# Threshold attention and a feed-forward block on one core: weight masks on VectorE, small copies on ScalarE, transposes ahead of the products with v, and two extra products a slot

## The chip, the cores and the metric

The kernel runs on one core of a Trainium2 chip. The metric is the device time of one execution in microseconds (us); lower is better. For profiled executions I also quote the span, which is some 2 us shorter than the time.

## The reference

Eight batches, eight heads, 576 rows of 64. Attention keeps the scores that lie within tau of the row's maximum. Its output is laid out as rows of 512 and goes through a normalised feed-forward block with 2048 hidden features.

```python
scores = scale * np.matmul(q, k.transpose(0, 1, 3, 2))
thresh = np.max(scores, axis=-1, keepdims=True) - tau
scores = np.where(scores >= thresh, scores, -1000000000.0)
scores = scores - np.max(scores, axis=-1, keepdims=True)
attn = np.exp(scores)
attn = attn / (np.sum(attn, axis=-1, keepdims=True) + 1e-09)
attn_out = np.matmul(attn, v)
# ... x = attn_out as rows of 512 ...
xn = (x - mu) / np.sqrt(var + 1e-06) * g_ln
out = x + np.maximum(xn @ w_ch1, 0.0) @ w_ch2
```

The feed-forward weights arrive as float64, which the kernel reads as pairs of 32-bit words and turns into float32 itself, in 32 chunks of 512 columns.

## The kernel before

The work is cut into **units** (one batch, two heads) of five **slots** (128 rows of queries each; the fifth has the last 64 rows of both heads). There are 32 units and 160 slots, numbered from 0. The program order is fixed by hand: `at_point(3 * n + i, ...)` hangs a piece of work on a point of slot n.

```python
for u in range(len(units)):
    for j in range(PTS):                     # five slots
        scs = scores(u, j)                   # TensorE
        es, thr = exponentials(scs)          # VectorE maximum, ScalarE exp
        conversion.carry()
        run(3 * n)                           # what hangs on this point
        ...
        weights(scs, es, thr)                # VectorE masking, GpSimd scaling
        conversion.end()                     # weight chunk: last step
        run(3 * n + 1)
        ...
        conversion.begin(2 if 20 <= n < 24 else 1)
        if blocks:                           # batches 1 to 7: through DRAM
            at_point(3 * n + 4, ...)         # turn_blocks: et -> scr
            if j in (1, 3, 4):
                at_point(3 * n + 7, ...)     # fetch: scr -> em, er
                at_point(3 * n + 12, ...)    # values_of: pv
        else:                                # batch 0: TensorE transposes
            at_point(3 * n + 3, turn_weights, u, j, es)
            if j in (1, 3, 4):
                at_point(3 * n + 6, lambda u=u, j=j: values_of(u, j, rounds.pop(u)))
        n += 1
```

In batch 0 (slots 0 to 19) the attention weights are transposed on TensorE (tile tp, and tr for the last 64 columns), then copied to em and er:

```python
def turn_weights(u, j, es):
    # ... em, er, tr allocated ...
    for h in range(2):
        # ... four transposes into tp, one into tr ...
        nc.scalar.copy(em[:, h, :, o : o + 128], tp)
    for h in range(2):
        # ...
        nc.vector.tensor_copy(er[r, o : o + 128], tr[r, h])
```

In the other seven batches VectorE transposes blocks into et, four DMAs carry et to a scratch tensor in DRAM (scr), and others bring it back as em and er. All these DMAs are issued by one queue, SyncE's. The products pv (v with em, then with er) wait for that round trip.

A weight chunk goes through ScalarE (Square, Sign and a scaled Identity) and is finished by GpSimd with a product. Three small constants serve that.

```python
g_sb = consts.tile([128, NK], F32, name="g_sb")
g_half = consts.tile([128, NK], F32, name="g_half")
half_sb = consts.tile([128, 1], F32, name="half_sb")
tiny_sb = consts.tile([128, 1], F32, name="tiny_sb")
ident = consts.tile([128, 128], F32, name="ident")
# ... weights, then the pools ins (q, k, v) and att (e, em, er, et) behind ...
```

## Time and profile before

| | before |
|---|---|
| median of 3 runs | 1567.52 us (1562.31 to 1567.53) |
| span of the profiled run | 1561.5 us |
| TensorE busy | 1477.1 us, 95% |
| mean granted TensorE clock | 0.965 of full |
| slots 0 to 25 (210.86 us) | loop of waits, clock 0.76 from 8 to 170 us |
| from slot 26 on (1339.9 us) | TensorE full, clock 1.00 |

First TensorE's timeline ahead of slot 13, a fourth slot of its unit (start us, duration us, engine, line, operation, tiles, count; in brackets the idle time before and what ended it; in all timelines here, lines between those shown are left out):

```profile
106.47 3.46 PE L416 MATMUL pv<-em,v_in 128*64 128x256 f32 x16
109.76 0.60 PE L416 MATMUL pv<-er,v_rest 128*64 128x256 f32 x4
112.70 0.30 PE L347 MATMUL tr<-ident,e 128*64 128x128 f32 x1 [1.75 <-ACT x L427]
```

and VectorE's in that slot:

```profile
113.58 0.59 DVE L354 COPY er<-tr 64x128 f32<-64x128 f32 x2 [2.00 <-PE tr L349]
114.20 0.82 DVE L309 SCALAR_TENSOR_TENSOR e<-sc,thr,e 128x576 f32<-128x576 f32 x1
```

The product pv goes first, ScalarE carries it out, only then can tr be written (1.75 us of waiting), and VectorE, whose small copy stands ahead of the masking in its queue, waits 2.00 us for tr. The next scores wait for the masking. Over the first 240 us that wait is (us in total, times, longest):

```profile
PE sc L278 <- DVE e L309: 37.1, 23, 3.9
```

### The profile page before, as it was taken

The numbers are of one execution on the slowest core, as the hardware profiler recorded it, in microseconds if no ns is written. First come the engines' busy times: TensorE is split into PE (matmuls) and PEld (weight loads), VectorE is DVE, ScalarE is ACT, GpSimd is POOL, SyncE is SP. The second block draws the span as 40 slices with busy tenths as digits, with TensorE's granted clock in tenths as the row PEclk, the third lists the DMA queues.
The fourth block names the chain that finished last, engine by engine and source line by source line (L and its number), as shares of the span: only waits on it lengthen the run. The fifth ranks groups of instructions, "written<-read, shape, count | busy, mean of one in ns | idle before, by whom it ended". The sixth has DMA issues, their size and how long they took to land.

```text
span 1561.5 us, 17868 instructions
## 1 busy us (share of the span) xinstructions
PE 1477.1 (95%) x5686; PEld 714.8 (46%) x5686; DVE 808.6 (52%) x1548; ACT 460.8 (30%) x786; POOL 513.9 (33%) x774
## 2 busy tenths in 40 slices
PE   5777699999999999999999999999999999999998
PEld 3444344444444444444444444444444444444443
DVE  5666676666556655665566555655656551001001
ACT  5666664212321232123211421133113320210200
POOL 4656673333223322333233323332333222100000
PEclk8867599999999999999999999999999999999999
DMA  5333387787667776777667767776777665001001
GB/s 141 96 87 94 106 199 165 166 182 163 152 156 173 165 167 152 161 152 190 141 150 167 162 156 159 157 174 150 159 154 169 149 139 121 7 3 17 7 7 20
DMA packets 701452, 204.37 MB, mean 131 GB/s; under 512 B 632752, under 2 KB 697264, under 8 KB 701360
## 3 DMA queue, kind: packets, MB, share of 16 engines
q1 hardware_dynamic: 698960, 202.95, 57.1%
q8 instruction: 46, 0.75, 0.2%
q10 hardware_dynamic: 2368, 0.30, 0.1%
q14 instruction: 46, 0.38, 0.1%
q0 software_dynamic: 32, 0.00, 0.0%
HBM read 119.41 MB, written 83.76 MB: 130 GB/s over the span
## 4 chain that ended last, share of the span: by engine, by line
PE 79%; SPq 6%; DVE 5%; DMA 4%; POOL 2%; ACT 2%; issue 2%; POOLq 0%; DVEq 0%; ACTq 0%
PE p L494 31%; PE p L536 26%; PE pv L416 10%; PE sc L278 10%; DMA em<-scr 4%; DVE e L309 2%; SPq L103 2%; SPq L479 1%; SPq L372 1%; ACT e L297 1%; PE tp L338 1%; SPq L117 1%; DVE neg L290 1%; SPq L121 1%; POOL w L230 1%
## 5 line engine op out<-in xcount | busy, mean ns | idle before, releaser
L494 PE MATMUL p<-xc,w 128*128 128x512 f32 x1152 | 518.6, 600 | 12.5 <-DVE xc L455 9.8
L536 PE MATMUL p<-hidden,w 128*128 128x512 f32 x1152 | 513.1, 597 | 0.0
L297 ACT ACTIVATE e<-sc,neg 128x576 f32<-128x576 f32 x288 | 199.9, 737 | 602.7 <-DVE neg L290 588.5
L290 DVE TENSOR_REDUCE neg<-sc 128x1 f32<-128x576 f32 x288 | 206.2, 751 | 309.7 <-PE sc L278 309.0
L494 PEld LDWEIGHTS p<-xc,w 128*128 128x128 f32 x1152 | 213.1, 190 | 270.0 <-issue 244.9
L536 PEld LDWEIGHTS p<-hidden,w 128*128 128x128 f32 x1152 | 214.2, 190 | 263.2 <-issue 260.5
L315 POOL TENSOR_SCALAR e<-e,den 128x576 f32<-128x576 f32 x288 | 218.3, 764 | 257.1 <-DVE den L313 241.1
L309 DVE SCALAR_TENSOR_TENSOR e<-sc,thr,e 128x576 f32<-128x576 f32 x288 | 225.4, 816 | 70.4 <-ACT e L297 69.0
L293 POOL TENSOR_SCALAR thr<-neg,low_sb 128x1 f32<-128x1 f32 x288 | 76.0, 264 | 501.2 <-DVE neg L290 500.3
L278 PE MATMUL sc<-kT,qT 64*128 64x288 f32 x1024 | 188.3, 459 | 39.4 <-DVE e L309 30.9
L501 ACT ACTIVATE hidden<-p 128x512 f32<-128x512 f32 x144 | 86.0, 598 | 352.6 <-PE p L494 352.5
L416 PE MATMUL pv<-em,v_in 128*64 128x256 f32 (+1 forms) x1536 | 167.1, 353 | 6.1 <-DMA em<-scr 5.9
L278 PEld LDWEIGHTS sc<-kT,qT 64*128 64x128 f32 x1024 | 103.2, 198 | 148.8 <-issue 93.7
L365 DVE STREAM_TRANSPOSE et<-e 128x1152 f32<-128x1152 f32 x112 | 152.9, 1365 | 0.5
L416 PEld LDWEIGHTS pv<-em,v_in 128*64 128x64 f32 x1536 | 93.6, 145 | 85.4 <-issue 43.4
L471 POOL TENSOR_TENSOR o<-o,x 128x512 f32<-128x512 f32 x36 | 45.7, 1268 | 216.5 <-DVE o L470 216.5
L470 DVE TENSOR_TENSOR o<-p,rb 128x512 f32<-128x512 f32 x36 | 24.6, 683 | 161.5 <-PE p L536 150.0
L416 PE MATMUL pv<-er,v_rest 128*64 128x256 f32 (+1 forms) x384 | 54.3, 332 | 0.0
L510 POOL TENSOR_TENSOR ss<-ss,sq 128x512 f32<-128x512 f32 x27 | 34.4, 1273 | 60.1 <-ACT sq L508 60.1
L427 ACT COPY x<-pv 128x256 f32<-128x256 f32 (+3 forms) x120 | 32.0, 288 | 46.3 <-PE pv L416 42.9
L278 PE MATMUL sc<-kT,q_diag 128*128 128x288 f32 x128 | 37.7, 418 | 6.3 <-DVE e L309 6.2
L255 DVE STREAM_TRANSPOSE qT<-q_in 128x256 f32<-128x256 f32 x56 | 21.6, 423 | 41.6 <-POOL q_in L248 41.6
(68 smaller groups left out, 694.6 us busy)
## 6 DMA issues: line engine op xcount, KB each, us to landing
scr<-et SPq DMA_DIRECT2D x224, 288.0 KB, 4.4
em<-scr SPq DMA_DIRECT2D x112, 512.0 KB, 5.0
hidden<-in_moe_w_ch_dram SPq DMA_DIRECT2D x32, 512.0 KB, 3.8
q_in<-in_q_dram SPq DMA_DIRECT2D x128, 72.0 KB, 4.3
out_dram<-ot SPq DMA_DIRECT2D x144, 64.0 KB, 1.9
k_in<-in_k_dram SPq DMA_DIRECT2D x124, 72.0 KB, 2.6
v_in<-in_v_dram SPq DMA_DIRECT2D x64, 128.0 KB, 3.6
scr_rest<-et SPq DMA_DIRECT2D x112, 72.0 KB, 4.6
```

The source lines that it names most:

```text
L278: nc.tensor.matmul(sc[:, c, :HALF], lhsT=lhsT, rhs=kT[rows, c * HALF : (c + 1) * HALF], start=True, stop=True,)
L290: nc.vector.tensor_reduce(out=neg[:, i : i + 1], in_=sc[:, :, :HALF], axis=AXL.XY, op=ALU.max, negate=True)
L293: nc.gpsimd.tensor_scalar(out=thr[:, i : i + 1], in0=neg[:, i : i + 1], scalar1=-1.0, scalar2=low_sb, op0=ALU.mult, op1=ALU.add,)
L297: nc.scalar.activation(es[:, i].rearrange("p (c n) -> p c n", c=2), sc[:, :, :HALF], func=AF.Exp, bias=neg[:, i : i + 1],)
L309: nc.vector.scalar_tensor_tensor(out=e2, in0=sc[:, :, :HALF], scalar=thr[:, i : i + 1], in1=e2, op0=ALU.is_ge, op1=ALU.mult, accum_out=den ...
L315: nc.gpsimd.tensor_scalar(out=es[:, i], in0=es[:, i], scalar1=den[:, i : i + 1], scalar2=1.0, op0=ALU.mult, op1=ALU.mult,)
L365: nc.vector.transpose(et[:, :, :, j % 2], es.rearrange("p h (n c) -> p h n c", c=32))
L416: nc.tensor.matmul(pv[64 * h : 64 * h + 64, :n], lhsT=vt[:, c, h, :] if c < J else vr[:, h, :], rhs=em[:, h, c, :n] if c < J else er[:, :n ...
L471: nc.gpsimd.tensor_tensor(out=o, in0=o, in1=groups[g][:, m], op=ALU.add)
L494: nc.tensor.matmul(p1, lhsT=w1_sb[c][:, d * 128 : (d + 1) * 128], rhs=xc[:, c, :], start=(c == 0), stop=(c == NK - 1),)
L501: nc.scalar.activation(hidden[:, d], p1, func=AF.Relu)
L536: nc.tensor.matmul(p2, lhsT=w2_sb[d][:, m * 128 : (m + 1) * 128], rhs=hidden[:, d], start=(d == 0), stop=(d == ND - 1),)
```

## The change

The intent is to relieve GpSimd and ScalarE of the weight masks, to end VectorE's wait for tr, and to keep TensorE's clock up in the first 21 slots. One VectorE comparison-and-multiply replaces Sign, Identity and GpSimd's product. The er copies move to ScalarE. In batch 0, pv moves behind the slot's transposes (point 3n+7 for 3n+6). Two products of 128x512 whose result is never read end each of slots 0 to 20. The three small constants go, since nothing uses them.

```diff
-    g_half = consts.tile([128, NK], F32, name="g_half")
-    half_sb = consts.tile([128, 1], F32, name="half_sb")
-    tiny_sb = consts.tile([128, 1], F32, name="tiny_sb")
 ...
-            nc.scalar.activation(y, y, func=AF.Sign, bias=tiny_sb)
-            nc.scalar.activation(y, y, func=AF.Identity, scale=gh, bias=gh)
 ...
-            nc.gpsimd.tensor_tensor(out=chunks[i][0], in0=a, in1=y, op=ALU.mult)
+            dst, _, gi = chunks[i]
+            nc.vector.scalar_tensor_tensor(
+                out=dst if gi is None else a, in0=y, scalar=(1.0625 * 2.0**-15) ** 2, in1=a,
+                op0=ALU.is_ge, op1=ALU.mult,
+            )
+            if gi is not None:
+                nc.gpsimd.tensor_scalar(
+                    out=dst, in0=a, scalar1=g_sb[:, gi : gi + 1], scalar2=1.0,
+                    op0=ALU.mult, op1=ALU.mult,
+                )
 ...
-                nc.vector.tensor_copy(er[r, o : o + 128], tr[r, h])
+                nc.scalar.copy(er[r, o : o + 128], tr[r, h])
 ...
+    def keep_busy(u):
+        idle = ps_ff.tile([128, TOK], F32, tag="ff", name="idle")
+        for _ in range(2):
+            nc.tensor.matmul(
+                idle, lhsT=avg_sb, rhs=turned[u][1][:, :TOK], start=True, stop=True,
+            )
 ...
+            if n < 21:
+                keep_busy(u)
 ...
-                    at_point(3 * n + 6, lambda u=u, j=j: values_of(u, j, rounds.pop(u)))
+                    at_point(3 * n + 7, lambda u=u, j=j, tw=rounds_at: values_of(u, j, tw[0]))
```

More of the change, by code (lines that the diff above doesn't have):

```diff
@@ L136 @@
     nc.vector.memset(avg_sb, 1.0 / DM)
-    nc.vector.memset(half_sb, 0.5)
-    nc.vector.memset(tiny_sb, -(1.0625 * 2.0**-15) ** 2)
     nc.vector.tensor_scalar(
@@ L151 @@
     nc.gpsimd.dma_start(out=g_sb, in_=g_ln.rearrange("(c p) -> p c", p=128))
-    nc.gpsimd.tensor_scalar(
-        out=g_half, in0=g_sb, scalar1=0.5, scalar2=1.0, op0=ALU.mult, op1=ALU.mult
-    )
     WC = 512
@@ L214, in begin @@
             )
-            gi = chunks[i][2]
-            gh = half_sb if gi is None else g_half[:, gi : gi + 1]
-            nc.scalar.activation(y, y, func=AF.Sign, bias=tiny_sb)
-            nc.scalar.activation(y, y, func=AF.Identity, scale=gh, bias=gh)
             made[i] = (a, y, r)
@@ L353, in turn_weights @@
                 o = (j % 2) * 128
-                nc.vector.tensor_copy(er[r, o : o + 128], tr[r, h])
+                nc.scalar.copy(er[r, o : o + 128], tr[r, h])
             else:
-                nc.vector.tensor_copy(er[r, :64], tr[r, h, r])
+                nc.scalar.copy(er[r, :64], tr[r, h, r])
+        return em, er, n
     def turn_blocks(u, j, es):
@@ L671 @@
             else:
-                at_point(3 * n + 3, turn_weights, u, j, es)
+                rounds_at = []
+                at_point(
+                    3 * n + 3,
+                    lambda u=u, j=j, es=es, tw=rounds_at: tw.append(turn_weights(u, j, es)),
+                )
                 if j in (1, 3, 4):
-                    at_point(3 * n + 6, lambda u=u, j=j: values_of(u, j, rounds.pop(u)))
+                    at_point(3 * n + 7, lambda u=u, j=j, tw=rounds_at: values_of(u, j, tw[0]))
             n += 1
```

## The prediction

> **What bounds the kernel now.** I read the page's forty slices first, then three long stretches cut where the slices change, then the groups of instructions of the first 240 us, and last the timeline of single slots. The slices:
>
> ```profile
> PE   5777699999999999999999999999999999999998
> DVE  5666676666556655665566555655656551001001
> PEclk8867599999999999999999999999999999999999
> ```
>
> TensorE is full from the sixth slice on; in the first five it is neither full nor at full clock. The stretches (columns: length, then busy time with instruction counts of PE, PEld, DVE, ACT, POOL, then clock, DMA share, GB/s):
>
> ```profile
> 8.46:166.85 158.39, 115.92 (x557) 70.72 (x557) 104.96 (x232) 102.30 (x167) 97.28 (x119) 0.76 0.39 106
> 166.85:209.63 42.78, 27.15 (x82) 12.59 (x82) 30.73 (x56) 27.25 (x43) 28.53 (x32) 0.71 0.48 135
> 209.63:1561.50 1351.87, 1334.04 (x5048) 631.48 (x5048) 670.77 (x1253) 329.98 (x576) 384.98 (x611) 1.00 0.60 134
> ```
>
> The third stretch is 1334.04 of 1351.87 us busy at clock 1.00: it is matmuls in a fixed order, and the change adds none there. Only the first two, 201 us, can move. Nobody is full in them, so a loop of waits sets the pace, and the groups name it:
>
> ```profile
> L278 PE MATMUL sc<-kT,qT 64*128 64x288 f32 x192 | 59.3, 593 | 39.4 <-DVE e L309 30.9 <-DVE qT L259 8.5
> L354 DVE COPY er<-tr 64x128 f32<-64x128 f32 x32 | 9.2, 288 | 25.4 <-PE tr L349 25.2
> L356 DVE COPY er<-tr 64x64 f32<-64x64 f32 x8 | 1.8, 222 | 11.8 <-PE tr L349 11.8
> L347 PE MATMUL tr<-ident,e 128*64 128x128 f32 x20 | 7.0, 349 | 10.2 <-ACT x L427 10.2
> ```
>
> Scores wait for the masking on VectorE (L309); VectorE in turn stood 25.4 + 11.8 = 37.2 us ahead of the small copies (er) for TensorE's transposes, which, where a product pv came before them in the slot, waited for ScalarE to carry pv out. A slot (VectorE's first maximum to the next slot's) is on average, over slots 5 to 19 by place in the unit of five: 7.6 (6.63, 9.54, 6.62), 7.4, 10.9 (this one ends with the transposes of the next unit's q and k), 7.2 and 5.0 us, 38.2 a unit.
>
> **What the Trainium skill says.** (1) "TensorE: Matmul & The Clock Gate", Part 1: the array runs at half clock unless a free-running window of 3413 ns was busy. The trace agrees: read by single microseconds the clock is 1.00 or 0.50, and all its changes in the first 220 us lie on one grid of 3.413 us. (2) The same page's Part 4 says transposes do not count as busy. The trace disagrees: a window of transposes and little else kept the clock,
>
> ```profile
> 147.27:150.69 3.42, 1.77 (x14) 1.03 (x10) 1.42 (x3) 2.33 (x5) 1.78 (x3) 1.00 0.00 0
> 130.21:133.62 3.41, 0.94 (x7) 0.71 (x7) 1.56 (x5) 3.07 (x7) 3.41 (x5) 0.98 0.00 0
> 188.23:191.64 3.41, 3.17 (x4) 1.17 (x4) 3.41 (x6) 0.93 (x2) 3.41 (x4) 0.52 0.81 284
> ```
>
> while 0.94 us (second line) lost it: the next window is at 0.50. Over all windows to 220 us I fit, as an estimate, some 1.25 us of full-array work to keep the clock, with the scores of 64 rows counting about half; to win it back a window must be nearly full (third line, 3.17 us of 128x512 products, then warm). (3) "SBUF — State Buffer", section "SBUF: two separate sides": a VectorE operation with two SBUF inputs and a GpSimd operation exclude each other on a shared port. The trace agrees: L206 takes 0.69 us alone and 1.11 us beside L315. (4) "PSUM — Partial Sum Buffer", "Engine vs sequencer instructions": ScalarE's queue is strictly first in, first out. The trace shows every em copy after that slot's exponentials; this decides the sign below.
>
> **The change part by part.** *Mask.* ScalarE loses two operations a chunk (0.72 + 0.81 us), 32 times; it is not on the loop. GpSimd loses the product w (1.33 us) and gets a one-input scaling for the 16 w1 chunks (est. 0.7 us, from L315's 0.76 for 576). VectorE gets one two-input operation of 512: like L206, est. 1.1 us beside L315, and it is on the loop, once per chunk. *Small copies.* VectorE loses 0.59 us a slot and the wait before it. Its own loop is then maximum 1.42, exponential 0.21 more, masking 1.56, reciprocal with gaps 0.3, weight mask 1.1, next chunk 0.42 + 1.1: 6.0 us; with the turn of q and k 9.25; 5.05 for the single-sided fifth slot. *Idle products.* Each is two records of 128x512; L494's fourteen records in 6.17 us give 0.44 us a record in a stream, so two products are 1.75 us warm and about twice that cold. *Order.* In a slot TensorE now has scores, transposes, pv, idle products, next scores. pv takes the PSUM buffer of the slot's first transposes (rings of two, taken in order of first use; the wait of tr for x above confirms that order), so it waits for the em copy, which stands behind both exponentials. From the maximum N: exponentials end at N+2.1, em copy N+2.7, pv from N+2.75, 2.2 us warm, idle 1.75, scores 1.24 and 0.25 to reach VectorE: N+8.2 (N+7.9 ahead of the fifth slot, whose scores are shorter; N+6.75 where pv is the 64-column one).
>
> Before pv TensorE now stands idle: about 6 us in the fourth slot (maximum late after the turn), 3.5 in the first, 1.5 in the second. By the window rule the first two start pv cold, the fourth always, the first four times in five; the 7.7 us of pv and idle products end it after 3.4 to 6.8 us, mean 5.1, of which half is lost: 2.5 us x 1 and 2.4 x 0.8 = 1.9; the second slot 0.3.
>
> | slot in unit | before | after |
> |---|---|---|
> | 1st, pv 256 | 7.6 | 8.2 + 1.9 = 10.1 |
> | 2nd, pv 64 | 7.4 | 6.75 + 0.3 = 7.05 |
> | 3rd, turn | 10.9 | 9.25 |
> | 4th, pv 256 | 7.2 | 7.9 + 2.5 = 10.4 |
> | 5th | 5.0 | 5.05 |
> | unit | 38.2 | 41.85 |
>
> Three units: 3 x 3.7 = +11. The first unit was 34.1 us and has one pv slot: I get 36.6, +2.5. Slot 20 was 12.6 (VectorE waited for GpSimd's product w, and pv was cold) and becomes 10.1: -2.5. Slot 21 was 11.4 and becomes 3.2 + 0.3 + two masks 2.2 + a transpose 1.36 + two chunks 2.65 = 9.7: -1.7, because the waits of 2 to 3 us for w are gone. From slot 22 to 209.63 two masks more a slot (+2.2 each) against waits removed come out even, and the cold stretch after the 3.2 us gap at 206 should go: -3. Later masks may cost 1. Sum: 11 + 2.5 - 2.5 - 1.7 - 3 + 1 = +7 us.
>
> **Rivals.** (a) VectorE becomes the loop and pv hides: 6.0 + 6.0 + 9.25 + 6.0 + 5.05 = 32.3 us a unit, 3 x 5.9 = 18 us less; with 3 less in the first unit, slot 20 at 7.25 (5.4 less) and the same 3.7 after it, about 1538. For it: the 37.2 us of waits are real. Against: pv and idle products (3.95 us) follow the exponentials in the first and fourth slots and end after VectorE is ready. (b) The clock stays low, because the gaps outlast windows: cold pv slots run 2.75 + 4.2 + 3.5 + 2.5 = 13 us, others 2 us more, some 10 us a unit, 1607. For it: the gaps of 3.5 and 6 us. Against: the idle products alone are 3.5 us cold and follow pv, a full window. (c) The products warm the array everywhere, without loss: 37.2 us a unit, about 1558. (d) The masks (12 after slot 20) delay the first FFN group: VectorE is 30.73 of 42.78 us busy there; up to 5 us more.
>
> **Range and chances.** The sum gives 1567.5 + 7 = 1574. Rivals (a) and (c) mark 1538 and 1558, (b) 1607; the window phase is luck, and runs of before spread by 5 us. Eight in ten: 1550 to 1595. Faster than 1536 would need all of rival (a) and a little more: 0.05. Slower than 1599 needs most of (b): 0.07. Within 2%: 0.88.
>
> **What would show it.** In the changed kernel: no VectorE wait for tr; pv waiting for ScalarE's em in the first, second and fourth slots, some 2 us each or more; idle products of about 0.6 us records when warm, 1.1 cold; VectorE masks near 1.1 us; mean clock of the first stretch around 0.8; the third stretch unchanged within 3 us. The prediction is wrong if pv does not wait for em, if the clock stays at 0.5 in spite of the products, or if the last 1350 us move.

## More of the kernel before

The prediction shows the slices, the stretches and the groups. Two more views make its argument visible.

Second, what SyncE's queue waited for from 240 to 1300 us (us in total, times, longest), which the prediction did not look at, although the page that it read counts 6% of the span for SyncE's queue and 4% for the DMAs of em in the chain of work that ended last:

```profile
SPq L372 <- DVE et L365: 104.3, 35, 7.2
SPq L394 <- DMA scr<-et: 53.8, 30, 3.8
```

and TensorE's wait for the round trip from 240 us to the end:

```profile
PE pv L416 <- DMA em<-scr: 5.9, 9, 1.5
```

and how long its DMAs took in that stretch (tiles, queue, count, KB each, median us from issue to landing):

```profile
scr<-et SPq DMA_DIRECT2D x212, 288.0 KB, 4.4
em<-scr SPq DMA_DIRECT2D x106, 512.0 KB, 4.9
...
q_in<-in_q_dram SPq DMA_DIRECT2D x100, 72.0 KB, 4.4
```

The queue had 104.3 us in which it stood ready before VectorE had finished et. So it ran ahead of its producer, and TensorE hardly waited for it.

## The result, and the profile after

| | before | after |
|---|---|---|
| median of 4 runs | 1567.53 us (1562.31 to 1568.90) | 1589.62 us (1585.82 to 1595.02) |
| span of the profiled run | 1561.5 us | 1586.8 us |
| mean clock | 0.965 | 0.979 |

The ratio is 1.015 (95% interval 1.0112 to 1.0188). Ratios here are the mean time of one kernel's runs over that of the other's of the same rounds, so not quite the ratio of the medians. The time lies inside the predicted range, 16 us above the predicted point.

The slices after, to be held against the prediction's first fence:

```profile
PE   5777699989999999999999999999999999999998
DVE  5666886655556655665566555565555552000001
PEclk9888799999999999999999999999999999999999
```

The clock is higher in most of the first five slices, and TensorE's row from the sixth slice on looks as full as before but for one 8. Slices are too coarse for more. Two stretches of each kernel, cut at the same times (columns as in the prediction), before:

```profile
8.00:170.00 162.00, 119.08 (x568) 72.38 (x570) 107.70 (x237) 104.42 (x170) 99.37 (x122) 0.76 0.38 104
240.00:1300.00 1060.00, 1052.00 (x4283) 503.98 (x4282) 626.56 (x1182) 282.52 (x495) 336.66 (x564) 1.00 0.72 161
```

and after:

```profile
8.00:170.00 162.00, 122.91 (x616) 67.73 (x616) 105.16 (x211) 77.48 (x162) 92.64 (x117) 0.89 0.40 101
240.00:1300.00 1060.00, 1034.97 (x4221) 496.61 (x4218) 615.89 (x1162) 281.51 (x492) 328.10 (x553) 1.00 0.72 158
```

The first stretch went from clock 0.76 to 0.89. The second line of each is the surprise: in the same 1060 us TensorE got 4221 products done where it had done 4283, and was idle 25.03 us where it had been idle 8.00. To see how the whole span splits, I took the starts of VectorE's maxima, one per slot:

| profiled run, us | before | after | difference |
|---|---|---|---|
| start to slot 0's maximum | 10.78 | 12.29 | +1.5 |
| slots 0 to 25 | 210.86 | 211.31 | +0.4 |
| from slot 26's maximum to the end | 1339.9 | 1363.2 | +23.3 |
| span | 1561.5 | 1586.8 | +25.3 |

**The first 26 slots**, where all the edits lie but the masks of the last three weight chunks, came out even. By place in the unit, over slots 5 to 19, they are now 9.92, 6.67, 8.79, 10.29 and 4.63 us, 40.3 a unit. TensorE's waits in the first 240 us show the loop that the prediction described:

```profile
PE pv L414 <- ACT em L338: 26.1, 7, 5.5
PE pv L414 <- ACT em L340: 9.1, 4, 2.3
PE sc L275 <- DVE e L306: 1.9, 1, 1.9
```

The wait of the scores for the masking is down from 37.1 to 1.9 us. In its place pv waits 35.2 us for ScalarE's em copies. Slot 13 again, on TensorE:

```profile
110.22 0.27 PE L346 MATMUL tr<-ident,e 128*128 128x128 f32 x1
116.03 3.68 PE L414 MATMUL pv<-em,v_in 128*64 128x256 f32 x16 [5.53 <-ACT em L338]
119.49 1.07 PE L414 MATMUL pv<-er,v_rest 128*64 128x256 f32 x4
120.49 2.52 PE L593 MATMUL idle<-kT,avg_sb 128*128 128x512 f32 x4
122.84 1.13 PE L275 MATMUL sc<-kT,q_diag 128*128 128x288 f32 x4
```

on ScalarE:

```profile
114.13 1.37 ACT L294 ACTIVATE e<-sc,neg 128x576 f32<-128x576 f32 x2 [4.93 <-DVE neg L287]
115.39 1.07 ACT L338 COPY em<-tp 128x512 f32<-128x512 f32 x2
116.33 0.54 ACT L351 COPY er<-tr 64x128 f32<-64x128 f32 x2
```

and on VectorE:

```profile
116.65 0.67 DVE L219 SCALAR_TENSOR_TENSOR hidden<-hidden 128x512 f32<-128x512 f32 x1
124.02 0.76 DVE L287 TENSOR_REDUCE neg<-sc 128x1 f32<-128x576 f32 x1 [5.29 <-PE sc L275]
```

TensorE has the transposes done at 110.5, stands idle 5.53 us until the em copy behind both exponentials, then runs pv, the two unread products (2.52 us) and the next scores. VectorE waits 5.29 us for those scores. No wait of VectorE for tr is left.

**The rest** lost 23.3 us, where nothing was edited but those three masks. TensorE's wait for the DRAM round trip from 240 us on, which had been 5.9 us:

```profile
PE pv L414 <- DMA em<-scr: 23.9, 17, 4.4
```

and what SyncE's queue waited for from 240 to 1300 us:

```profile
SPq L392 <- DMA scr<-et: 66.0, 30, 3.8
SPq L370 <- DVE et L363: 52.6, 21, 5.6
```

The queue's spare time ahead of VectorE fell from 104.3 to 52.6 us, and it stood 66.0 us instead of 53.8 for its own stores to land. Its DMAs took, in the same stretch,

```profile
scr<-et SPq DMA_DIRECT2D x206, 288.0 KB, 5.1
em<-scr SPq DMA_DIRECT2D x104, 512.0 KB, 4.9
...
q_in<-in_q_dram SPq DMA_DIRECT2D x100, 72.0 KB, 5.0
```

So the stores of et went from 4.4 to 5.1 us and the loads of q_in from 4.4 to 5.0, while em came back as fast as before. The stores became slower, the queue fell behind, and products waited. The order of SyncE's issues is the same in both programs, and so is each other engine's order in these batches, those masks apart. What does differ in the built program is where tiles lie. Each of the three removed constants had taken 32 bytes of every partition, and everything behind them moved down by 96: et from byte 163,200 to 163,104, q_in from 118,144 to 118,048. Before, these tiles start 128 bytes past a multiple of 256; after, 32 bytes past one.

### The profile page after: what moved, and what is told of

Its sections match the earlier page's. It is cut to its first block, busy times and chain, and to the rows that moved or that the text cites. A ratio compares the mean times of both kernels' runs of the same rounds, so it can differ in the third digit from the quotient of the medians.

```text
span 1586.8 us, 17999 instructions
## 1 busy us (share of the span) xinstructions
PE 1490.2 (94%) x5770; PEld 714.6 (45%) x5770; DVE 815.5 (51%) x1538; ACT 420.7 (27%) x762; POOL 497.5 (31%) x757
## 4 chain that ended last, share of the span: by engine, by line
PE 80%; DMA 7%; DVE 5%; SPq 4%; ACT 2%; issue 1%; POOL 1%; POOLq 0%; ACTq 0%; DVEq 0%
PE p L534 28%; PE p L492 28%; PE pv L414 12%; PE sc L275 9%; DMA em<-scr 6%; DVE neg L287 2%; SPq L477 2%; PE idle L593 1%; ACT e L294 1%; DVE e L306 1%; SPq L392 1%; SPq L396 1%; DVE hidden L198 0%; SPq L370 0%; PE var L512 0%
## 5 line engine op out<-in xcount | busy, mean ns | idle before, releaser
L312 POOL TENSOR_SCALAR e<-e,den 128x576 f32<-128x576 f32 x288 | 231.5, 810 | 226.7 <-DVE den L310 209.2
L414 PE MATMUL pv<-em,v_in 128*64 128x256 f32 (+1 forms) x1536 | 171.8, 355 | 62.4 <-DMA em<-scr 27.0
L275 PE MATMUL sc<-kT,qT 64*128 64x288 f32 x1024 | 164.2, 434 | 11.9 <-DVE qT L256 10.0
L275 PEld LDWEIGHTS sc<-kT,qT 64*128 64x128 f32 x1024 | 91.5, 188 | 122.2 <-issue 80.5
L414 PE MATMUL pv<-er,v_rest 128*64 128x256 f32 (+1 forms) x384 | 58.9, 345 | 0.0
L593 PE MATMUL idle<-kT,avg_sb 128*128 128x512 f32 x84 | 44.1, 650 | 0.0
```

Source lines behind the costliest of these rows:

```text
L275: nc.tensor.matmul(sc[:, c, :HALF], lhsT=lhsT, rhs=kT[rows, c * HALF : (c + 1) * HALF], start=True, stop=True,)
L312: nc.gpsimd.tensor_scalar(out=es[:, i], in0=es[:, i], scalar1=den[:, i : i + 1], scalar2=1.0, op0=ALU.mult, op1=ALU.mult,)
L414: nc.tensor.matmul(pv[64 * h : 64 * h + 64, :n], lhsT=vt[:, c, h, :] if c < J else vr[:, h, :], rhs=em[:, h, c, :n] if c < J else er[:, :n ...
L593: nc.tensor.matmul(idle, lhsT=avg_sb, rhs=turned[u][1][:, :TOK], start=True, stop=True,)
```

## The experiments

Two theories for the 23 us stood against each other. **Addresses:** the 96-byte shift slows the DMAs. **Timing:** the reshaped first stretch leaves the later queue in a worse phase, and the addresses do not matter. For the first stretch the question was which of the four parts gain and which lose. All twelve kernels gave correct results, each timed in three rounds.

One table serves all (spans in us; "offset" is how far past a multiple of 256 bytes the q, k, v tiles and the e, em, er, et tiles start):

| kernel | offset q,k,v / em,et | to first maximum | slots 0 to 25 | from slot 26 | median us |
|---|---|---|---|---|---|
| before | 128 / 128 | 10.78 | 210.86 | 1339.9 | 1567.53 |
| after | 32 / 32 | 12.29 | 211.31 | 1363.2 | 1589.62 |
| e1 | 128 / 128 | 10.81 | 209.03 | 1340.6 | 1564.39 |
| e2 | 160 / 160 | 12.15 | 215.54 | 1368.0 | 1596.29 |
| e3 | 128 / 128 | 10.71 | 190.33 | 1340.3 | 1544.29 |
| e4 | 128 / 128 | 10.79 | 185.39 | 1340.4 | 1539.65 |
| e5 | 128 / 128 | 10.80 | 187.59 | 1338.8 | 1539.89 |
| e6 | 128 / 128 | 10.92 | 214.39 | 1341.1 | 1568.23 |
| e7 | 128 / 128 | 10.82 | 172.49 | 1341.7 | 1528.48 |
| e8 | 64 / 64 | 12.20 | 211.64 | 1361.4 | 1586.36 |
| e9 | 32 / 128 | 12.25 | 208.97 | 1339.9 | 1567.04 |
| e10 | 128 / 160 | 10.87 | 210.76 | 1365.6 | 1588.44 |
| e11 | 0 / 0 | 10.77 | 173.84 | 1327.5 | 1513.54 |
| e12 | 128 / 128 | 10.69 | 201.60 | 1340.2 | 1554.69 |

The medians of before were 1562.9 (e1 to e4), 1563.27 (e5 to e8) and 1563.36 (e9 to e12).

### e1_after_pad96: the changed kernel with the old addresses

```diff
     g_sb = consts.tile([128, NK], F32, name="g_sb")
+    filler = consts.tile([128, 24], F32, name="filler")
 ...
+    nc.vector.memset(filler[:, 0:1], 0.0)
```

> The changed kernel with 96 bytes of filler in the place of the three small constants that the change removed, so that every SBUF tile lies at the address that it had before (a multiple of 64 bytes) instead of 96 bytes lower (32 past a multiple of 64). Theory A (addresses): the 18 us more of waits of pv for em after 240 us come from transfers slowed by the shifted tiles; expected 1570 us (1565 to 1576), waits for em after 240 us back from 24 to some 6 us, landing of q_in and k_in back from 4.4 to 3.6 us. Theory B (timing: the new first batch puts the later slots into another phase against the transfers): no change, 1586 to 1595 us.

Measured: 1564.39 us, just under the expected range; ratio to before 1.001 (0.9983 to 1.0037). A tile of 96 bytes that nothing reads took 1.4% off the changed kernel. Slots 0 to 24 are the changed kernel's to a few hundredths (units of 34.5, 41.0, 41.0 and 39.0 us), so the timing into the later batches is the same, and the loss there is gone. It is gone from slot 25 too: in the changed kernel pv waits 2.07 us for em there and the slot takes 8.86 us, here 1.06 and 6.48. TensorE's wait for the round trip from 240 us on:

```profile
PE pv L416 <- DMA em<-scr: 5.9, 7, 1.4
```

and SyncE's queue from 240 to 1300 us:

```profile
SPq L372 <- DVE et L365: 105.4, 34, 7.1
SPq L394 <- DMA scr<-et: 54.5, 30, 3.5
```

Both are as before the change. The timing theory falls.

One rival needs a look at the traces: that the engines themselves are slower at shifted tiles. They are not. From 240 to 1500 us the median record of pv with em is 379 ns and that of the long transposes into et 1369 ns in e1, in the changed kernel, in e10 and in e11 alike. Only the longest pv records differ, 431 ns in e1 and 689 in the changed kernel.

### e2_before_shift32: the kernel before, moved by 32 bytes

```diff
+    filler = consts.tile([128, 8], F32, name="filler")
 ...
+    nc.vector.memset(filler[:, 0:1], 0.0)
```

> The kernel before with 32 bytes of filler among the constants, so that its tiles lie 32 past a multiple of 64 bytes, with no other change. Theory A (addresses): some 16 to 22 us slower than before, 1583 to 1590 us, through waits of pv for em after 240 us. Theory B (timing): the same as before, 1562 to 1569 us.

Measured: 1596.29 us, ratio 1.0198 (1.0156 to 1.024). The old program without any of the change loses 33 us by its addresses alone, more than the 16 to 22 expected: 28.1 from slot 26 on, 4.7 in the first 26 slots, 1.4 at the start. Its four runs spread from 1587.8 to 1597.72 us and the profiled one is the slowest, so these parts are on the high side. The wait for the round trip:

```profile
PE pv L418 <- DMA em<-scr: 22.0, 20, 2.6
```

### e8_after_pad32: multiples of 64, but not of 128

The edit is e2's filler of 32 bytes, in the changed kernel.

> The changed kernel with 32 bytes of filler: its tiles lie at a multiple of 64 bytes, but 64 past a multiple of 128, whereas e1 and the kernel before lie at a multiple of 128. If what matters is a multiple of 64, 1562 to 1568 us as e1; if it is 128, so that the 128-byte pieces of q and k cross a boundary as they do 32 past, 1582 to 1592 us as the changed kernel; in between if only part of the transfers care.

Measured: 1586.36 us, ratio 1.0149 (1.0125 to 1.0173), and 19.8 us of waits for the round trip. A multiple of 64 is not enough; this costs what the changed kernel costs.

### e9_after_qkv_shift and e10_after_att_shift: which tiles

The first leaves the constants and q, k, v at the changed kernel's offset and puts 96 bytes behind them. The second is e1 with 32 bytes behind q, k, v.

```diff
 # e9
+    filler2 = ins.tile([128, 24], F32, tag="filler2", bufs=1, name="filler2")
 # e10: e1's filler, and
+    filler2 = ins.tile([128, 8], F32, tag="filler2", bufs=1, name="filler2")
```

> The changed kernel with a filler of 96 bytes behind q, k and v: the constants, q, k and v stay 32 past a multiple of 64 bytes as in the changed kernel, the tiles behind them (e, em, er, et, x, o) lie at a multiple of 128 as before. If the loads of q, k and v in pieces of 128 bytes carry the cost, 1582 to 1592 us and q_in landing in 4.9 us; if the round trip of the weights (et out, em in) carries it, 1562 to 1568 us and q_in alone slow; between them if both count.

> The reverse of e9: the constants, q, k and v at the addresses of before, the tiles of the round trip (e, em, er, et) and x, o 32 past a multiple of 64. If the round trip carries the cost, 1582 to 1592 us with et landing in 4.9 us instead of 4.5; if the loads of q, k, v carry it, 1562 to 1568 us. The two differences of e9 and e10 from e1 should add up to some 25 us if they act alone.

Measured: e9 1567.04 us, ratio 1.0027 (1.0001 to 1.0053); e10 1588.44 us, ratio 1.0175 (1.0142 to 1.0208). In e9 the loads of q_in are slow (median 4.9 us), and only at the start does it show: the first maximum comes 1.4 us late. The other 23 us (1589.62 to 1567.04) sit in what lies behind the filler, the tiles of the round trip among it. In e10 the wait for it is

```profile
PE pv L416 <- DMA em<-scr: 21.8, 19, 3.9
```

and the DMAs from 240 to 1300 us are

```profile
scr<-et SPq DMA_DIRECT2D x205, 288.0 KB, 5.1
em<-scr SPq DMA_DIRECT2D x104, 512.0 KB, 4.8
...
q_in<-in_q_dram SPq DMA_DIRECT2D x100, 72.0 KB, 4.4
```

The sum closes. The group of pv with em in e1 is

```profile
L416 PE MATMUL pv<-em,v_in 128*64 128x256 f32 (+1 forms) x1536 | 165.7, 350 | 44.2 <-ACT em L340 26.1
```

and in e10

```profile
L416 PE MATMUL pv<-em,v_in 128*64 128x256 f32 (+1 forms) x1536 | 175.9, 360 | 60.7 <-ACT em L340 26.1
```

which is 10.2 us more busy and 16.5 more idle, 26.7 together, and the spans differ by 26.8. The second filler also moves qT and kT, which lie behind q, k, v, then e, er, x and the rest, and I did not separate et, which the DMAs read, from em and er, which they write. That em landed in 4.7 to 5.1 us at every offset, while et's stores went from 4.5 (e1) to 5.1, and that the output's stores took 1.9 us in e1 and 2.0 in e10, speaks for et, but does not show it.

### e3_after_pad_noidle: without the unread products

```diff
-            if n < 21:
-                keep_busy(u)
```

> The padded changed kernel without the products that nothing reads. Theory W (they keep the clock up and pay for themselves): slower than e1 by 5 us or more, clock of the first batch back near 0.7. Theory C (they stand behind pv on the loop and cost their own 1.75 us or more in the first, second and fourth slots of a unit while the clock they buy is mostly used by themselves): faster than e1 by 2 to 10 us, a unit near 39 us against 40.9.

Measured against e1: 1544.29 us for 1564.39, so the unread products cost 20 us, twice what the better guess allowed, although without them the clock from 8 to 170 us is 0.79 instead of 0.89. They are on the loop (pv, products, next scores), and what they earn in clock is less than what they take: the second place in the unit falls from 6.67 to 5.38 us, the first from 9.92 to 6.87.

### e4_after_pad_first: the products with v first again

```diff
-  at_point(3 * n + 7, lambda u=u, j=j, tw=rounds_at: values_of(u, j, tw[0]))
+  at_point(3 * n + 6, lambda u=u, j=j, tw=rounds_at: values_of(u, j, tw[0]))
```

> The padded changed kernel with the old order: products with v ahead of the transposes. If the wait of pv for the em copy behind the exponentials is what eats the gain, as the prediction says, this wait (35 us in the first 180 us) goes, VectorE sets the pace and a unit takes 32 to 35 us instead of 40.9: 24 to 36 us less than e1, some 1535 to 1546 us under theory A. Rival: the wait of tr for the copy of x comes back and takes its place, and the time stays within 8 us of e1.

Measured: 1539.65 us, ratio 0.9853 (0.9827 to 0.9879), 25 us better than e1. No wait of pv for em is left. What replaces it is the old one of the transposes for pv's way out:

```profile
PE tr L346 <- ACT x L427: 20.1, 11, 4.0
```

It is longer than before (10.2 us in the group that the prediction shows), but VectorE no longer hangs on it, because the er copy behind it is now ScalarE's.

### e5_before_er, e6_before_mask and e12_before_order: one part alone

Each is the kernel before with one part of the change and no other: er copies to ScalarE; the mask to VectorE (the three constants still allocated); transposes ahead of pv.

> The kernel before with one part of the change alone: the small copies (er) on ScalarE instead of VectorE; addresses as before. VectorE's 37 us of waits for tr and its 11 us of copies go; ScalarE then has some 6.2 us a slot (exponentials 1.4, em 1.1, er 0.5, pv 0.3, four operations of the weights 2.9) and becomes the pace. Expected: a unit of 32 to 35 us instead of 38 and 1540 to 1552 us. Rival: the wait only moves (TensorE's transposes still stand between two scores), unit above 36 and the time within 8 us of before.

> The kernel before with the weight mask on VectorE alone; addresses as before. If the mask lies on the loop in full, 0.7 us for 20 slots and two of 1.05 in the slots 21 to 24, less the waits for w there: 5 to 12 us slower, some 1568 to 1575. If VectorE does it while it would wait for tr anyway, the slots stay as they are and the removed waits for w in slots 20 to 24 give 2 to 8 us: 1555 to 1562.

> The kernel before with the new order alone (transposes ahead of products with v; small copies on VectorE, mask and addresses as before, no idle products). VectorE then waits for the transposes only, not for pv and x, but pv waits for em behind the exponentials and stands ahead of the next scores. If the two cancel, 1556 to 1572 us with a unit of 36 to 39 us; if pv's wait is worse than the wait for tr was, above 1572; if better, below 1556.

Measured: 1539.89 us, ratio 0.9856 (0.9834 to 0.9879); 1568.23 us, ratio 1.0032 (1.0009 to 1.0055); 1554.69 us, ratio 0.9954 (0.9932 to 0.9976). So er alone gives 23 us, the mask alone costs 5, and the order alone gives 9. The order alone is good because in the old kernel VectorE waits for tr, and with transposes first that wait ends earlier: in the first 240 us it fell from 37.0 to 4.5. Once er is off VectorE the reason is gone, and the same order costs 16 us (e3 against e7). The parts do not add.

### e7_after_pad_first_noidle: only what gains

Mask and er as in the change, pv first, no unread products, old addresses.

> The padded changed kernel with products first and without the idle products (mask and er as changed). Theory C again (they only cost): faster than e4 by 2 to 8 us, 1532 to 1538, with the places of 7.8 us in e4's units (fourth slot) down to some 6. Theory W (in this order TensorE has room, so they cost nothing and hold the clock): slower than e4 by 3 to 15 us, with the clock of the first batch at 0.75 against 0.89.

Measured: 1528.48 us, ratio 0.9785 (0.9761 to 0.9808). That is 11 us under e4, where at most 8 were expected, so the unread products cost time with pv first as well. The slots by place are 5.37, 5.93, 8.78, 5.37 and 4.82 us, 30.3 a unit, and VectorE is the loop: in the first 210 us its longest entries are

```profile
DVE e L308 <- ACT e L296: 6.8, 19, 0.9
DVE qT L258 <- POOL q_in L247: 6.2, 3, 2.1
DVE neg L289 <- PE sc L277: 4.9, 3, 2.0
```

In this company the mask on VectorE is worth 11 us (e5's 1539.89 to 1528.48), although alone it cost 5.

### e11_first_noidle_256: the same, every tile on a multiple of 256

Two of the small constants share one tile, which frees one more 32 bytes and brings all offsets to 0.

```diff
-    tau_sb = consts.tile([128, 1], F32, name="tau_sb")
-    scl_sb = consts.tile([128, 1], F32, name="scl_sb")
+    ts_sb = consts.tile([128, 2], F32, name="ts_sb")
+    tau_sb, scl_sb = ts_sb[:, 0:1], ts_sb[:, 1:2]
```

> e7 with its tiles at a multiple of 256 bytes (two one-element constants share a tile, no filler) instead of 128 past one. If a boundary of 256 bytes counts too, as the table of beats in the Trainium skill's DMA page would have it for the 256-byte pieces of et, et and scr land sooner than in 4.5 us and the time falls below e7, 1518 to 1526 us; if 128 bytes is all that counts, 1526 to 1532 us as e7.

Measured: 1513.54 us (1512.90 to 1515.17), ratio 0.9688 (0.9668 to 0.9708): faster than both kernels, by 50 us in the medians than before, and below the 1518 to 1526 expected. From slot 26 on it takes 1327.5 us where the eight kernels with offset 128 / 128 took 1338.8 to 1341.7. The group of pv has next to no wait left:

```profile
L414 PE MATMUL pv<-em,v_in 128*64 128x256 f32 (+1 forms) x1536 | 153.8, 338 | 1.3 <-DMA em<-scr 1.2
```

with et stored in a median of 4.2 us and q_in loaded in 4.2.

## Why the prediction was right or wrong

**Its range held by luck: the time was lost where it had ruled a loss out.** It forecast 6 us more in the first 26 slots and 1 later; the spans show 0.4 there, 1.5 before them and 23.3 later. By its own list of signs it was wrong ("if the last 1350 us move"). Two errors of opposite sign and a range 45 us wide kept the time inside. Without the address shift (e1) the first 26 slots came out 8 us below their predicted sum; the shift, which it did not see, added about 26 us to the span (1560.4 to 1586.8).

- *What bounds the kernel: right for the first stretch.* The waits that it named vanished (VectorE for tr: 37.2 us to none; scores for masking: 37.1 us to 1.9), and pv's wait for em came as it said, in the first, second and fourth slots, 35.2 us in eleven waits: about 5.5, 2.3 and 1.5 us each in the fourth, first and second slot, for the 6, 3.5 and 1.5 that it gave.
- *The slot table: right, a little too long.* Predicted 10.1, 7.05, 9.25, 10.4 and 5.05, measured 9.92, 6.67, 8.79, 10.29 and 4.63: 40.3 a unit for 41.85, which is 4.6 us too much over three units. The first unit took 34.5 for 36.6 (2.1), slot 20 took 8.24 for 10.1 (1.9), slot 21 9.69 for 9.7, and slots 22 to 25 came out even (38.08 us before, 38.02 after). Of the 3 us that it hoped to gain beyond slot 21, 2.4 are there once the addresses are back (35.65 us in e1); in the changed kernel the wait for em in slot 25 took them. So its 6 us for this stretch (its sum of 7 without the later masks' 1) were 0.4 in the changed kernel, and -1.8 in e1, which has no address shift.
- *The term most mis-sized there was the mask.* It was put at 1.1 us beside GpSimd's scaling. The trace has, for the sixteen chunks of w1 (nanoseconds, minimum/median/maximum),

```profile
L219 DVE SCALAR_TENSOR_TENSOR hidden<-hidden x16: 670/672/673, 20.5 to 141.9; 128x512 f32<-128x512 f32 x16
```

  In slot 13 it starts right behind the reciprocal at 116.65 us, and GpSimd starts scaling at 116.94; that this order is why it stays short is argued, not shown. It is 0.43 us less for each mask on the loop; the fifth slot had been put 0.42 us too long and the third 0.46.
- *The clock: better than said.* 0.89 for "around 0.8". The unread products averaged 650 ns a record over 84 (median 593), so most met a warm array by its own sign of about 0.6 us warm and 1.1 cold.
- *The failed step: "the third stretch unchanged within 3 us".* It was 23.3 us longer from slot 26 on, and TensorE's wait for em from 240 us on went from 5.9 to 23.9 us. The argument was that these are matmuls in a fixed order, and the order was indeed unchanged. What it left out is that taking three constants away moves every later tile. e1 put 96 bytes back and this stretch went to 1340.6 us, e2 moved the old kernel by 32 bytes and it went to 1368.0. In time the shift is 22 us by the two ratios (1.015 and 1.001), 25 by the medians.
- *The rivals.* None of the four is what happened; (c) would have been 37.2 us a unit. Rival (a), VectorE as the loop at about 1538, was ruled out for the right reason, since pv and the unread products did end after VectorE was ready. e7 takes both reasons away and is that rival: 30.3 us a unit for its 32.3, and 1528.48 us. (The parts of its plain VectorE slot add up to 6.1 us, not 6.0.) Rival (b), the cold clock, did not come. Of (d), a delay at the first feed-forward groups, nothing shows in e1's 1340.6.

What stays open is how an address slows the DMAs. "DMA: Bandwidth & Descriptors", section "How a descriptor splits into AXI transactions", says that transactions start on 256-byte boundaries and that bytes read before a descriptor's start are wasted. A row of et goes out in pieces of 256 bytes, so by that account a piece takes, as an estimate, 8 beats at offset 0, 9 at 32, 10 at 64, 12 at 128 and 13 at 160. The best place, offset 0, agrees (1327.5 us from slot 26 on). The order of the others does not: offset 128 took 1338.8 to 1341.7, while 32, 64 and 160 took 1363.2, 1361.4 and 1365.6 to 1368.0. The page cannot be the whole account, and no run here tells what is.

## What to carry to other kernels

Before trusting "nothing changes there", compare where the tiles lie in the two built programs: on this kernel deleting 96 bytes of constants cost as much as the best part of the change gained, and filler or a shared tile gave it back. A product that only keeps the clock up is not free: on the loop it cost 20 us here although the clock rose, and 11 with pv first. No run here has a place where it paid. Test parts of a change in each other's company too, because the order that gained 9 us alone cost 16 once another part had removed its reason.

## What the Trainium skill lacked or had wrong

- "SBUF — State Buffer", section "Operand start alignment", treats alignment as a matter of legality and says that its runs timed nothing. These runs give the time: tiles of a DMA round trip (and those behind them) at offsets of 32, 64 or 160 bytes past a multiple of 256 instead of 128 cost 21 to 28 us from slot 26 on, and offset 0 instead of 128 saved 14.2 (e7 to e11). The median landing of the stores of et was 5.0 to 5.4 us at offsets 32, 64 and 160, 4.3 to 4.5 at 128 and 4.2 at 0.
- "DMA: Bandwidth & Descriptors", section "How a descriptor splits into AXI transactions": its beats would put offset 32 (estimate 9) ahead of offset 128 (estimate 12). The runs have it the other way round, 1363.2 us against 1339.9 for the same program order. As it is the only account there of what a start address costs a plain DMA, it should say that 128 did better here.
- "TensorE: Matmul & The Clock Gate", Part 4, says that the full clock does not engage for transposes, which do not count as busy "the same way". For keeping the clock the kernel before disagrees: the window from 147.27 to 150.69 us, whose 1.77 us of TensorE work is transposes but for some 0.3 us of pv, was followed by no loss of clock, while the next one, with 1.37 us of little but scores, was. For winning it back the page may hold: the window from 153.94 to 157.35 us, 3.39 us busy, most of it with transposes, did not bring the full clock, and 3.02 us of 128x512 products from 188.07 to 191.49 did.
- The same page's Part 1 describes how the clock is won, which the grid of 3.413 us confirms, but not that winning it can cost more than it brings: 0.79 to 0.89 in clock for 20 us more time (e3 to e1).
